# Hedgehog attention and a gated MLP on one core: projections on half rows of the array, and the tails' first layer with the tokens as weights

## The chip, the cores and the metric

The kernel runs on one NeuronCore of one Trainium2 chip. The metric is the device time of one execution in microseconds, the median of several. Three runs of the kernel before took 282.17, 283.19 and 283.45 us; the median is 283.19 us. The core has a tensor engine (PE, with its weight loads listed as PEld), VectorE (DVE), ScalarE (ACT), GpSimd (POOL) and SyncE (SP, which here only issues DMAs). A matmul takes its stationary operand from a weight load (`lhsT`), streams the moving operand (`rhs`) and writes into PSUM, of which this kernel uses eight buffers, one bank each.

## The reference, cut to what matters

There are 8 batches, 8 heads, 576 tokens, a head dimension of 64, 128 features, a model width of 512 and an inner width of 1024.

```python
def phi(x):
    proj = np.einsum('bhsd,df->bhsf', x, w_phi)
    proj = proj - np.max(np.abs(proj), axis=-1, keepdims=True)
    return np.concatenate([np.exp(proj), np.exp(-proj)], axis=-1)
q_p, k_p = phi(q), phi(k)
kv = np.einsum('bhsf,bhsd->bhfd', k_p, v);  z = np.sum(k_p, axis=2)
num = np.einsum('bhsf,bhfd->bhsd', q_p, kv)
den = np.einsum('bhsf,bhf->bhs', q_p, z)[..., None] + 1e-06
x = (num / den).transpose(0, 2, 1, 3).reshape(B, S, H * D)
h = np.maximum(x @ w_in, 0.0)
u, v = h[..., :d_ff // 2], h[..., d_ff // 2:]
v_n = (v - mean(v)) / np.sqrt(var(v) + 1e-06)
v_s = np.einsum('ts,bsd->btd', w_spatial, v_n) + b_spatial[None, :, None]
out = (u * v_s) @ w_out
```

## The kernel before, in words

**Units.** Of the 576 tokens of a batch, 512 are taken as four blocks of 128 (`NB`), and the last 64 are a tail. The attention works in 36 units: 32 of two heads of one batch (`pair`), and four tail units, which hold the tails of two batches side by side, 64 rows each (`TL = 64`), for all eight heads. In each unit there are eight groups of 128 rows by 64 dimensions: two heads by four blocks, or eight heads of the tails.

**One unit.** The keys and queries of a unit are brought into transposed form (`kT`, `qT`): four tiles of 128 x 128, in which rows 0 to 63 hold the dimensions of one group and rows 64 to 127 those of the next. For batches from 2 on a DMA transposes them (`cross`), before that PE does (`a_transpose`). `by_token` (L263) multiplies them with `wphi2`, a block diagonal matrix of 128 x 256: `w_phi` stands in rows 0 to 63 of the left half and in rows 64 to 127 of the right half, and the rest is zero. So one matmul over all 128 rows gives the projections of two groups, and two matmuls fill a PSUM bank. `a_keys` (L270) takes the largest absolute value of each projection on DVE (L278) and both exponentials on ACT (L281). `a_queries` (L283) takes the queries' maxima (L292) and splits each into two bf16 numbers in `mhl`. `a_scale` makes the values times the exponentials of the keys' maxima (`vs`, POOL). Later steps of the same unit turn the maxima (`a_max_t`, L327), project the queries again by feature with the maxima taken off (`a_qfeat`, L344 to L365), sum keys and values (`a_kv`, L378 to L383), divide (`a_num`, L398, with L388 and L389) and turn the result into `xT` (`a_x_t`).

**The MLP.** For each batch `b_v` makes the `v` half of the first layer by token (`v_mm`, L447, with its evacuation L449 and statistics L450 and L451), `b_root` and `b_ln` normalize it (L461, L467), `b_u` makes the `u` half by feature (L534, L536), `b_s` does the spatial product and the gate (L543, L544, L546) and `b_o` the output product (`o_mm`, L568, L571). The tails of a batch go through the same steps in functions of their own. `b_v_tail` (L488) computes all eight 128-wide slices of the first layer for the 64 tail tokens, with the weights stationary and the tokens moving: 32 matmuls of 64 columns (L497). It evacuates the `v` slices to `vTt` (L499) and the `u` slices to `uTt` (L500). `b_turn_tail` (L502) turns `vTt` back with four transposes (L507), copies the result out of PSUM on DVE (L511) and takes its statistics (L512, L513).

**Order.** The program is written out step by step. Step i emits the stages of several units after one another (`ORDER`, with lags: the keys and queries of unit i, the sums of unit i-2, the attention of unit i-3, and so on). Behind the stages for keys, queries, sums and next, `fill` takes MLP tasks from a queue: each task has a cost, and each of these stages gives a share of a credit that follows from the length of the queue. `b_tasks` (L625) lists a batch's tasks in order. `load` and its relatives are emitted at given steps on the queues of SP and POOL. A scheduler then lays the instructions out for each engine and assigns the eight PSUM banks. It may move an instruction a few places. Each engine works through its own list in order.

**Around the change.** In step i the keys' four projections come first, then their readers, then MLP tasks for a credit share of 0.375, then the queries' four projections with their readers, and then MLP tasks for a share of 0.25. In PE's list that is the burst of the keys, one or two MLP groups, the burst of the queries, and a further group.

Of the kernel before, what the change touches and what calls it, by code (L numbers as in the profile page):

```python
# [8 lines left out]
FP32 = mybir.dt.float32  # L9
BF16 = mybir.dt.bfloat16  # L10
AF = mybir.ActivationFunctionType
ALU = mybir.AluOpType
AX = mybir.AxisListType
# [3 lines left out]
def kernel(  # L17
# [15 lines left out]
    nc = tc.nc  # L33

    B, H, S, D = q.shape
    F = w_phi.shape[1]
# [3 lines left out]
    P = 128  # L40
    KC = DM // P
# [3 lines left out]
    TL = S - T0  # L45
# [4 lines left out]
    cpool = ctx.enter_context(tc.tile_pool(name="const", bufs=1))  # L50
# [4 lines left out]
    s2 = ctx.enter_context(tc.tile_pool(name="stage_b", bufs=2))  # L55

    psum = ctx.enter_context(tc.tile_pool(name="psum", bufs=8, space=bass.MemoryType.PSUM))
# [14 lines left out]
    gs = {}  # L72
# [47 lines left out]
        pin(nc.sync.dma_start_transpose)(out=u[x + "T"], in_=src.rearrange("p h x -> p (h x)"))  # L120


    wphi_f = s2.tile([P, F], FP32, tag="ob", name="wphi_f", bufs=6)
    for i in range(2):
        pin(nc.scalar.dma_start)(out=wphi_f[i * D:(i + 1) * D, :], in_=w_phi)
    alloc(0)
# [12 lines left out]
    bias = cpool.tile([P, NB], FP32)  # L139
# [4 lines left out]
    ident = cpool.tile([P, P], BF16)  # L144
# [115 lines left out]
            u[x + "T"] = a1.tile([P, 4, P], BF16, tag="kT", name="kT") if x == "k" else qts[u["i"] % len(qts)]  # L260
            copy(out=u[x + "T"], in_=pt)

    def by_token(xT, half):  # L263
        ps = psum.tile([P, 4, F], FP32, tag="bank", name="ps")
        for x in range(2):
            nc.tensor.matmul(out=ps[:, 2 * x:2 * x + 2, :], lhsT=xT[:, 2 * half + x, :], rhs=wphi2,  # L266
                             start=True, stop=True)
        return ps

    def a_keys(u):  # L270

        u["mk"] = small.tile([P, H], FP32, tag="mk", name="mk")
        u["kf"] = feat.tile([P, 2, H, F], BF16, tag="kf" if u["pair"] else "kf_t", name="kf",
                            bufs=4 if u["pair"] else 2)
        for half in range(2):
            pk = by_token(u["kT"], half)
            hs = slice(4 * half, 4 * half + 4)
            nc.vector.tensor_reduce(out=u["mk"][:, hs], in_=pk, axis=AX.X, op=ALU.max,  # L278
                                    apply_absolute_value=True)
            for s, sc in ((0, 1.0), (1, -1.0)):  # L280
                nc.scalar.activation(out=u["kf"][:, s, hs, :], in_=pk, func=AF.Exp, bias=0.0, scale=sc)  # L281

    def a_queries(u):  # L283

        m, early = mhl[u["i"] % NM], u["i"] < EARLY
        if not early:
            mq = small.tile([P, H], FP32, tag="mq", name="mq")
        for half in range(2):
            pq = by_token(u["qT"], half)
            if early and half == 0:  # L290
                mq = pq[:, 0, 0:H]
            nc.vector.tensor_reduce(out=mq[:, 4 * half:4 * half + 4], in_=pq, axis=AX.X, op=ALU.max,  # L292
                                    apply_absolute_value=True)
        eng = nc.vector if early else nc.gpsimd
        eng.tensor_copy(out=m[:, 0:H], in_=mq)
        eng.tensor_tensor(out=m[:, H:2 * H], in0=mq, in1=m[:, 0:H], op=ALU.subtract)

    def a_scale(u):
        em = small.tile([P, 2, H], FP32, tag="em" if u["pair"] else "em_t", name="em", bufs=3 if u["pair"] else 1)
# [144 lines left out]
    def v_mm(lhs, dst, r, stats, mv):  # L444
        pv = psum.tile([P, HALF], FP32, tag="bank", name="pv")
        for kc in range(KC):
            nc.tensor.matmul(out=pv[r], lhsT=lhs(kc), rhs=w_in_bf[:, kc, HALF:DFF],  # L447
                             start=(kc == 0), stop=(kc == KC - 1))
        nc.scalar.activation(out=dst[r], in_=pv[r], func=AF.Relu, bias=0.0, scale=1.0)  # L449
        nc.vector.bn_stats(out=stats[r], in_=dst[r])  # L450
        nc.vector.bn_aggr(out=mv[r], in_=stats[r])  # L451
# [35 lines left out]

    def b_v_tail(g, bls):  # L488
        d = gs[g]
        if bls[0] == 0:  # L490
            d["uTt"] = s2.tile([P, KC, P], BF16, tag="uTt", name="uTt", bufs=2)
        d["vTt"] = s2.tile([P, KC, TL], BF16, tag="vr", name="vTt", bufs=5)
        r = slice(bls[0] * TL, (bls[-1] + 1) * TL)
        pu = psum.tile([P, 2 * KC, TL], FP32, tag="bank", name="pu")
        for dc in range(2 * KC):
            for kc in range(KC):
                nc.tensor.matmul(out=pu[:, dc, :], lhsT=w_in_bf[:, kc, dc * P:(dc + 1) * P],  # L497
                                 rhs=d["xTt"][:, kc, r], start=(kc == 0), stop=(kc == KC - 1))
        nc.scalar.activation(out=d["vTt"], in_=pu[:, KC:2 * KC, :], func=AF.Relu, bias=0.0, scale=1.0)  # L499
        nc.scalar.activation(out=d["uTt"][:, :, r], in_=pu[:, 0:KC, :], func=AF.Relu, bias=0.0, scale=1.0)  # L500

    def b_turn_tail(g, bls):  # L502
        d = gs[g]
        r = slice(bls[0] * TL, (bls[-1] + 1) * TL)
        pt = psum.tile([P, KC, P], BF16, tag="bank", name="pt")
        for dc in range(KC):
            nc.tensor.transpose(out=pt[r, dc, :], in_=d["vTt"][:, dc, :], identity=ident)  # L507
        vr = s2.tile([P, HALF], BF16, tag="vr", name="vr", bufs=5)
        stats = small.tile([P, 6], FP32, tag="stats", name="stats")
        mv = small.tile([P, 1, 2], FP32, tag="mv_t", name="mv_t")  # L510
        nc.vector.tensor_copy(out=vr[r], in_=pt[r].rearrange("p n e -> p (n e)"))  # L511
        nc.vector.bn_stats(out=stats[r], in_=vr[r])  # L512
        nc.vector.bn_aggr(out=mv[r, 0, :], in_=stats[r])  # L513
        d["ln"] = vr, moments(mv, r, 1)

    def b_root_tail(g, bls):
# [11 lines left out]
    def b_u(b, dc):  # L528
        d = st[b]
        if dc == 0:  # L530
            d["uT"] = s2.tile([P, KC, T0], BF16, tag="uT", name="uT", bufs=1)
        pu = psum.tile([P, T0], FP32, tag="bank", name="pu")
        for kc in range(KC):
            nc.tensor.matmul(out=pu, lhsT=w_in_bf[:, kc, dc * P:(dc + 1) * P], rhs=d["xT"][:, kc, :],  # L534
                             start=(kc == 0), stop=(kc == KC - 1))
        nc.scalar.activation(out=d["uT"][:, dc, :], in_=pu, func=AF.Relu, bias=0.0, scale=1.0)  # L536

    def b_s(b, dc):
        d = st[b]
# [74 lines left out]
    MM = KC * T0 / 2400.0  # L614
# [10 lines left out]
    def b_tasks(b):  # L625

        g, bl = b // 2, b % 2
        outs = out_tasks(b - 1) if b else []
        vs = [(MM, lambda j=j: b_v(b, j)) for j in range(NB)]
        us = [(MM, lambda dc=dc: b_u(b, dc)) for dc in range(KC)]  # L630
        ss = [(MS, lambda dc=dc: b_s(b, dc)) for dc in range(KC)]
        ns = [(0.0, lambda j=j: b_ln(b, j)) for j in range(NB)]
        ts = outs[:1] + [(MM, lambda: b_v_tail(g, [bl]))] + vs[:2]
        ts += [(MM / 4, lambda: b_turn_tail(g, [bl]))] + outs[1:2] + vs[2:]
        ts += [(0.0, lambda: b_root_tail(g, [bl])), (0.0, lambda: b_ln_tail(g, [bl])), (0.0, lambda: b_root(b))]
        if b == 0:
            ts += [(0.3, lambda i=i: transpose_spatial(i)) for i in range(NB + 2)]
        for y in range(NB):
            ts += ns[y:y + 1] + outs[2 + y:3 + y] + us[y:y + 1]
        ts += ss  # L640
        ts.append((MS / 2, lambda: b_s_tail(g, [bl])))
        return ts + (out_tasks(b) if b == B - 1 else [])

# [26 lines left out]
    def step(i):  # L670

        if i == 0:
            a_transpose(units[0])
        left = [p - i + 1 for p in lists if p >= i]
        rate[0] = min(MOST, sum(cost for cost, _ in queue) / left[0]) if left else MOST
        for what, share in ORDER:
            for u in units[max(0, i - 5):i + 2]:
                if u["i"] + lag(u, what) != i or (what in ("sums", "attention", "out") and not u["pair"]):
                    continue
                last = u["pair"] and u["pj"] == NP - 1  # L680
                if what == "keys":
                    a_keys(u)
                    a_scale(u)
                elif what == "sums":
                    a_kv(u)
                elif what == "queries":
                    a_queries(u)
                elif what == "next":
                    a_transpose(u)
                elif what == "maxima":  # L690
                    a_max_t(u)
                elif what == "out":
                    a_x_t(u)
                    if last:
                        finish_batch(u, tail_x_t)
                        queue.extend(b_tasks(u["b"]))
                elif what == "features":
                    a_qfeat(u)
                elif what == "attention":
                    a_num(u)  # L700
                    if last:
                        finish_batch(u, tail_num)
            fill(share)
# [87 lines left out]
```

## Time and profile before

| | |
|---|---|
| median of three runs | 283.19 us |
| the profiled execution | 283.19 us, of which 281.4 us are the span from first to last instruction |
| busy share of the span | PE 92%, PEld 62%, DVE 86%, ACT 77%, POOL 65% |
| mean granted PE clock | 0.994 |
| 30 to 232 us | PE busy for 193.4 us, DVE 185.6, ACT 171.9, POOL 152.0 of 202 |
| 232 to 256 us | PE 24.0, DVE 16.2, ACT 12.3 of 24 |
| the projections L266 | 288 matmuls of 128 x 256, 272 ns each from start to end |
| the tails' first layer L497 | 256 matmuls of 128 x 64, 193 ns each from start to end |
| maxima L278, L292; exponentials L281 | 680 and 677 ns; 624 ns |

One execution was recorded. Each line of an instruction view has the start in us from the beginning of the span, the duration of the group in us, the engine, the line of the kernel, what is written and read, the shapes and the number of instructions; in brackets the engine's idle time before it and what ended it. A matmul line carries the part of the array that it uses as rows\*columns: 128\*128 is the whole array, 128\*64 half of its columns, 64\*128 half of its rows. Matmuls are pipelined, so one that takes 272 ns from start to end hands the array on long before: for throughput the distances from start to start count. The windows view gives, for a stretch, its length and then each engine's busy time, with the number of instructions in brackets, the granted PE clock, the DMA engines' share and GB/s. A line of the waits view has who waited for whom, then the sum in us, how many times, and the longest. The chain that ended last is the chain of work followed back from the last instruction, each step to what released it.

### The profile page before, as it was taken

To read this page: it belongs to the slowest core of one execution; us is meant where nothing else is said; L and a number is where in the kernel's file an instruction comes from. 1 tells how busy PE (TensorE), PEld (TensorE's weight loads), DVE (VectorE), ACT (ScalarE), POOL (GpSimd) and SP (SyncE) were. 2 spreads that over 40 slices of the span, in tenths; PEclk is the share of its full clock that TensorE was granted. 3 is DMA by queue.
4 is the path that set the end of the run, shared out by engine and by line. 5 is a ranking of instruction groups with operands and counts; after the bars stand their busy time and mean duration, and the time that the engine had idled before them with its cause. 6 is when DMAs were issued, how large, how long until landed. Compare 5 with 4: busy or idle time off the path is not lost.

```text
span 281.4 us, 8437 instructions
## 1 busy us (share of the span) xinstructions
PE 257.9 (92%) x3179; PEld 175.7 (62%) x3179; DVE 240.7 (86%) x623; ACT 217.0 (77%) x501; POOL 183.9 (65%) x312
## 2 busy tenths in 40 slices
PE   3769999999997999999997999999997999999993
PEld 2457877776764668666764667656864766555442
DVE  7978999989999899998889998997899797565752
ACT  6888998887896997888796979897896976723501
POOL 5897899899677954897677964897447740610200
PEclk9988999999999999999999999999999999999999
DMA  7989999999999996989789997989643300220115
GB/s 202 223 225 147 143 151 102 174 209 181 176 213 196 259 234 83 228 164 189 131 134 193 240 204 106 173 193 221 124 94 103 83 5 37 77 78 37 75 41 186
DMA packets 84985, 42.45 MB, mean 151 GB/s; under 512 B 51856, under 2 KB 80464, under 8 KB 84944
## 3 DMA queue, kind: packets, MB, share of 16 engines
q1 hardware_dynamic: 60240, 30.82, 50.4%
q0 software_dynamic: 24400, 10.89, 34.1%
q8 instruction: 25, 0.41, 0.6%
q10 hardware_dynamic: 304, 0.20, 0.2%
q14 instruction: 16, 0.13, 0.2%
HBM read 32.85 MB, written 9.44 MB: 150 GB/s over the span
## 4 chain that ended last, share of the span: by engine, by line
PE 58%; DVE 22%; ACT 8%; issue 4%; POOL 3%; DMA 2%; SPq 1%; ACTq 0%; POOLq 0%; DVEq 0%
PE ps L543 10%; PE pu L534 7%; PE po L568 7%; PE ps L266 6%; DVE mk L278 4%; DVE stats L450 4%; PE pv L378 4%; PE pv L447 4%; ACT kf L281 4%; PE pn L398 3%; PE ps L544 2%; PE pq L344 2%; PE pu L497 2%; DVE mq L292 2%; DVE x L389 2%
## 5 line engine op out<-in xcount | busy, mean ns | idle before, releaser
L306 POOL TENSOR_TENSOR vs<-v_f,em 128x512 bf16<-128x512 f32 x64 | 65.5, 1044 | 32.0 <-ACT em L301 31.8
L281 ACT ACTIVATE kf<-ps 128x512 bf16<-128x512 f32 x144 | 75.0, 624 | 11.2 <-DVE mk L278 10.8
L365 ACT ACTIVATE qf<-pq 128x512 bf16<-128x512 f32 x128 | 66.5, 618 | 9.6 <-PE pq L344 6.8
L278 DVE TENSOR_REDUCE mk<-ps 128x4 f32<-128x512 f32 x72 | 46.2, 680 | 1.2 <-PE ps L266 0.7
L292 DVE TENSOR_REDUCE mq<-ps 128x4 f32<-128x512 f32 x62 | 40.0, 677 | 0.8 <-PE ps L266 0.5
L543 PE MATMUL ps<-w_spT,vn 128*128 128x512 bf16 x128 | 33.3, 379 | 0.7 <-DVE vn L467 0.7
L568 PE MATMUL po<-w_out_bf,uT 128*128 128x512 bf16 x124 | 31.7, 379 | 2.0 <-ACT kf L281 1.2
L534 PE MATMUL pu<-xT,w_in_bf 128*128 128x512 bf16 x128 | 32.1, 379 | 0.0
L461 POOL TENSOR_TENSOR rs<-var,neghalf 64x1 f32<-64x1 f32 (+1 forms) x16 | 12.7, 795 | 29.3 <-DVE var L456 29.0
L447 PE MATMUL pv<-w_in_bf,xT 128*128 128x512 bf16 x128 | 31.5, 379 | 0.0
L450 DVE BATCH_NORM_STATS2 stats<-vr 128x6 f32<-128x512 bf16 x32 | 21.6, 682 | 7.8 <-ACT vr L449 7.7
L378 PE MATMUL pv<-vs,kf 128*128 128x66 bf16 x512 | 24.5, 193 | 3.8 <-ACT kf L281 3.1
L546 DVE TENSOR_TENSOR uT<-ps,uT 128x512 bf16<-128x512 f32 x32 | 21.5, 686 | 6.7 <-PE ps L544 5.4
L378 PEld LDWEIGHTS <-kf 128*128 128x128 bf16 x512 | 21.8, 97 | 7.0 <-issue 5.8
L536 ACT ACTIVATE uT<-pu 128x512 bf16<-128x512 f32 x32 | 19.5, 629 | 7.7 <-PE pu L534 5.1
L389 DVE TENSOR_TENSOR x<-pn,rc 128x256 bf16<-128x256 f32 x64 | 24.9, 418 | 0.4
L398 PEld LDWEIGHTS <-qf 128*128 128x128 bf16 x512 | 20.2, 97 | 6.1 <-ACT qf L365 0.4
L449 ACT ACTIVATE vr<-pv 128x512 bf16<-128x512 f32 x32 | 19.7, 624 | 5.4 <-PE pv L447 4.9
L380 PE MATMUL pv<-vst,kf 128*128 128x66 bf16 x128 | 21.2, 191 | 1.9 <-POOL vst L61 1.9
L398 PE MATMUL pn<-kv,qf 128*128 128x66 bf16 x512 | 21.8, 193 | 0.4 <-ACT qf L365 0.3
L467 POOL TENSOR_SCALAR vn<-vr,rs 128x512 bf16<-128x512 bf16 x28 | 21.3, 771 | 0.9
L571 ACT COPY ob<-po 128x512 f32<-128x512 f32 x17 | 10.2, 600 | 15.0 <-PE po L568 15.0
(137 smaller groups left out, 580.1 us busy)
## 6 DMA issues: line engine op xcount, KB each, us to landing
out_dram<-ob SPq DMA_DIRECT2D x31, 256.0 KB, 2.9
v_f<-in_v_dram SPq DMA_DIRECT2D x14, 512.0 KB, 6.1
k_bf<-in_k_dram POOLq DMA_DIRECT2D x14, 256.0 KB, 5.6
q_bf<-in_q_dram POOLq DMA_DIRECT2D x14, 256.0 KB, 5.4
qt<-qT_b SPq DMA_DIRECT2D x24, 64.0 KB, 4.3
out_dram<-ob SPq DMA_DIRECT2D x9, 128.0 KB, 2.8
v_tl<-in_v_dram SPq DMA_DIRECT2D x8, 128.0 KB, 6.3
v_f<-in_v_dram SPq DMA_DIRECT2D x1, 1024.0 KB, 8.8
```

The costliest lines, as they stand in the source:

```text
L278: nc.vector.tensor_reduce(out=u["mk"][:, hs], in_=pk, axis=AX.X, op=ALU.max, apply_absolute_value=True)
L281: nc.scalar.activation(out=u["kf"][:, s, hs, :], in_=pk, func=AF.Exp, bias=0.0, scale=sc)
L292: nc.vector.tensor_reduce(out=mq[:, 4 * half:4 * half + 4], in_=pq, axis=AX.X, op=ALU.max, apply_absolute_value=True)
L306: nc.gpsimd.tensor_tensor(out=vs[:, s, :, 0:D], in0=st[u["b"]]["v"][:, pj * H:(pj + 1) * H, :], in1=em[:, s, :].unsqueeze(2).to_broadcast( ...
L365: nc.scalar.activation(out=qf[:, s], in_=pq, func=AF.Exp, bias=0.0, scale=sc)
L378: nc.tensor.matmul(out=pv[:, hh, s, :], lhsT=u["kf"][:, s, 4 * hh + c, :], rhs=u["vs"][:, s, 4 * hh + c, :], start=(c == 0), stop=False)
L398: nc.tensor.matmul(out=pn[:, pos, :], lhsT=u["qf"][hh][:, s, pos, :], rhs=d["kv"][:, 2 * u["pj"] + hh, s, :], start=(s == 0), stop=(s == 1))
L447: nc.tensor.matmul(out=pv[r], lhsT=lhs(kc), rhs=w_in_bf[:, kc, HALF:DFF], start=(kc == 0), stop=(kc == KC - 1))
L450: nc.vector.bn_stats(out=stats[r], in_=dst[r])
L534: nc.tensor.matmul(out=pu, lhsT=w_in_bf[:, kc, dc * P:(dc + 1) * P], rhs=d["xT"][:, kc, :], start=(kc == 0), stop=(kc == KC - 1))
L543: nc.tensor.matmul(out=ps, lhsT=d["vn"][:, sp, cs], rhs=w_spT[:, sp, 0:T0], start=(sp == 0), stop=False)
L568: nc.tensor.matmul(out=po[r], lhsT=lhs(dc), rhs=w_out_bf[:, dc, :], start=(dc == 0), stop=(dc == KC - 1))
```

## The change

The projections of keys and queries of a unit are now issued in one burst ahead of all their readers (`a_project`). Each 128-row matmul of 256 columns becomes two matmuls of 64 rows and 128 columns: rows 0 to 63 with the left half of `wphi2`, rows 64 to 127 with the right half, in turn and into two PSUM banks, one for even and one for odd groups. The zero blocks are not multiplied any more. The readers work by bank and so by parity, with strided views. In a step the queries' readers stay where they were, behind the MLP tasks of the keys' share, while their projections stand before those tasks.

The tails' first layer is split into two parts. The `v` half takes the tokens as the stationary operand and goes through `v_mm` like the other blocks, into 64 rows of the bank, so that no turn is needed; `b_turn_tail` is gone. The `u` half becomes a task of its own (`b_u_tail`), ahead of the spatial products, and `uTt` has one buffer instead of two. In the list of tasks a cost of MM/4 is removed and one of MM/2 added. The float copy of `w_phi` gets its own place instead of a slot of the output buffers.

```diff
-    wphi_f = s2.tile([P, F], FP32, tag="ob", name="wphi_f", bufs=6)
+    wphi_f = cpool.tile([P, F], FP32)
...
-    def by_token(xT, half):
-        ps = psum.tile([P, 4, F], FP32, tag="bank", name="ps")
-        for x in range(2):
-            nc.tensor.matmul(out=ps[:, 2 * x:2 * x + 2, :], lhsT=xT[:, 2 * half + x, :], rhs=wphi2,
-                             start=True, stop=True)
+    def by_token(xT):
+        ps = [psum.tile([P, 4, F], FP32, tag="bank", name="ps") for _ in range(2)]
+        for j in range(4):
+            for y in range(2):
+                r = slice(y * D, (y + 1) * D)
+                nc.tensor.matmul(out=ps[y][:, j, :], lhsT=xT[r, j, :], rhs=wphi2[r, y * F:(y + 1) * F],
+                                 start=True, stop=True)
         return ps
+
+    def parity(t, y):
+        return t.rearrange("p (j two) -> p j two", two=2)[:, :, y]
+
+    def a_project(u):
+        u["pk"], u["pq"] = by_token(u["kT"]), by_token(u["qT"])
 
     def a_keys(u):
...
-        for half in range(2):
-            pk = by_token(u["kT"], half)
-            hs = slice(4 * half, 4 * half + 4)
-            nc.vector.tensor_reduce(out=u["mk"][:, hs], in_=pk, axis=AX.X, op=ALU.max,
+        for y, pk in enumerate(u["pk"]):
+            nc.vector.tensor_reduce(out=parity(u["mk"], y), in_=pk, axis=AX.X, op=ALU.max,
                                     apply_absolute_value=True)
             for s, sc in ((0, 1.0), (1, -1.0)):
-                nc.scalar.activation(out=u["kf"][:, s, hs, :], in_=pk, func=AF.Exp, bias=0.0, scale=sc)
+                nc.scalar.activation(out=u["kf"][:, s].rearrange("p (j two) f -> p j two f", two=2)[:, :, y, :],
+                                     in_=pk, func=AF.Exp, bias=0.0, scale=sc)
 
     def a_queries(u):
...
-        for half in range(2):
-            pq = by_token(u["qT"], half)
-            if early and half == 0:
-                mq = pq[:, 0, 0:H]
-            nc.vector.tensor_reduce(out=mq[:, 4 * half:4 * half + 4], in_=pq, axis=AX.X, op=ALU.max,
-                                    apply_absolute_value=True)
+        for y, pq in enumerate(u["pq"]):
+            nc.vector.tensor_reduce(out=mq[:, 4 * y:4 * y + 4], in_=pq, axis=AX.X, op=ALU.max, apply_absolute_value=True)
         eng = nc.vector if early else nc.gpsimd
-        eng.tensor_copy(out=m[:, 0:H], in_=mq)
-        eng.tensor_tensor(out=m[:, H:2 * H], in0=mq, in1=m[:, 0:H], op=ALU.subtract)
+        hi, lo = (m[:, e * H:(e + 1) * H].rearrange("p (j two) -> p two j", two=2) for e in range(2))
+        mq = mq.rearrange("p (two j) -> p two j", two=2)
+        eng.tensor_copy(out=hi, in_=mq)
+        eng.tensor_tensor(out=lo, in0=mq, in1=hi, op=ALU.subtract)
...
     def b_v_tail(g, bls):
         d = gs[g]
-        if bls[0] == 0:
-            d["uTt"] = s2.tile([P, KC, P], BF16, tag="uTt", name="uTt", bufs=2)
-        d["vTt"] = s2.tile([P, KC, TL], BF16, tag="vr", name="vTt", bufs=5)
         r = slice(bls[0] * TL, (bls[-1] + 1) * TL)
-        pu = psum.tile([P, 2 * KC, TL], FP32, tag="bank", name="pu")
-        for dc in range(2 * KC):
-            for kc in range(KC):
-                nc.tensor.matmul(out=pu[:, dc, :], lhsT=w_in_bf[:, kc, dc * P:(dc + 1) * P],
-                                 rhs=d["xTt"][:, kc, r], start=(kc == 0), stop=(kc == KC - 1))
-        nc.scalar.activation(out=d["vTt"], in_=pu[:, KC:2 * KC, :], func=AF.Relu, bias=0.0, scale=1.0)
-        nc.scalar.activation(out=d["uTt"][:, :, r], in_=pu[:, 0:KC, :], func=AF.Relu, bias=0.0, scale=1.0)
-
-    def b_turn_tail(g, bls):
...
-        for dc in range(KC):
-            nc.tensor.transpose(out=pt[r, dc, :], in_=d["vTt"][:, dc, :], identity=ident)
...
-        nc.vector.tensor_copy(out=vr[r], in_=pt[r].rearrange("p n e -> p (n e)"))
-        nc.vector.bn_stats(out=stats[r], in_=vr[r])
-        nc.vector.bn_aggr(out=mv[r, 0, :], in_=stats[r])
+        v_mm(lambda kc: d["xTt"][:, kc, r], vr, r, stats, mv[:, 0, :])
         d["ln"] = vr, moments(mv, r, 1)
...
+    def b_u_tail(g, bls):
+        d = gs[g]
+        if bls[0] == 0:
+            d["uTt"] = s2.tile([P, KC, P], BF16, tag="uTt", name="uTt", bufs=1)
+        r = slice(bls[0] * TL, (bls[-1] + 1) * TL)
+        pu = psum.tile([P, KC, P], FP32, tag="bank", name="pu")
+        for dc in range(KC):
+            for kc in range(KC):
+                nc.tensor.matmul(out=pu[:, dc, r], lhsT=w_in_bf[:, kc, dc * P:(dc + 1) * P],
+                                 rhs=d["xTt"][:, kc, r], start=(kc == 0), stop=(kc == KC - 1))
+        nc.scalar.activation(out=d["uTt"][:, :, r], in_=pu[:, :, r], func=AF.Relu, bias=0.0, scale=1.0)
...
-        ts = outs[:1] + [(MM, lambda: b_v_tail(g, [bl]))] + vs[:2]
-        ts += [(MM / 4, lambda: b_turn_tail(g, [bl]))] + outs[1:2] + vs[2:]
+        ts = outs[:1] + [(MM, lambda: b_v_tail(g, [bl]))] + vs[:2] + outs[1:2] + vs[2:]
...
-        ts += ss
+        ts += [(MM / 2, lambda: b_u_tail(g, [bl]))] + ss
...
                 if what == "keys":
+                    a_project(u)
                     a_keys(u)
                     a_scale(u)
```

More of the change, by code (lines that the diff above doesn't have):

```diff
@@ L274, in a_keys @@
                             bufs=4 if u["pair"] else 2)
-        for half in range(2):
-            pk = by_token(u["kT"], half)
-            hs = slice(4 * half, 4 * half + 4)
-            nc.vector.tensor_reduce(out=u["mk"][:, hs], in_=pk, axis=AX.X, op=ALU.max,
+        for y, pk in enumerate(u["pk"]):
+            nc.vector.tensor_reduce(out=parity(u["mk"], y), in_=pk, axis=AX.X, op=ALU.max,
                                     apply_absolute_value=True)
             for s, sc in ((0, 1.0), (1, -1.0)):
-                nc.scalar.activation(out=u["kf"][:, s, hs, :], in_=pk, func=AF.Exp, bias=0.0, scale=sc)
+                nc.scalar.activation(out=u["kf"][:, s].rearrange("p (j two) f -> p j two f", two=2)[:, :, y, :],
+                                     in_=pk, func=AF.Exp, bias=0.0, scale=sc)
     def a_queries(u):
         m, early = mhl[u["i"] % NM], u["i"] < EARLY
-        if not early:
+        if early:
+            mq = u["pq"][0][:, 0, 0:H]
+        else:
             mq = small.tile([P, H], FP32, tag="mq", name="mq")
-        for half in range(2):
-            pq = by_token(u["qT"], half)
-            if early and half == 0:
-                mq = pq[:, 0, 0:H]
-            nc.vector.tensor_reduce(out=mq[:, 4 * half:4 * half + 4], in_=pq, axis=AX.X, op=ALU.max,
-                                    apply_absolute_value=True)
+        for y, pq in enumerate(u["pq"]):
+            nc.vector.tensor_reduce(out=mq[:, 4 * y:4 * y + 4], in_=pq, axis=AX.X, op=ALU.max, apply_absolute_value=True)
         eng = nc.vector if early else nc.gpsimd
-        eng.tensor_copy(out=m[:, 0:H], in_=mq)
-        eng.tensor_tensor(out=m[:, H:2 * H], in0=mq, in1=m[:, 0:H], op=ALU.subtract)
+        hi, lo = (m[:, e * H:(e + 1) * H].rearrange("p (j two) -> p two j", two=2) for e in range(2))
+        mq = mq.rearrange("p (two j) -> p two j", two=2)
+        eng.tensor_copy(out=hi, in_=mq)
+        eng.tensor_tensor(out=lo, in0=mq, in1=hi, op=ALU.subtract)
     def a_scale(u):
@@ L489, in b_v_tail @@
         d = gs[g]
-        if bls[0] == 0:
-            d["uTt"] = s2.tile([P, KC, P], BF16, tag="uTt", name="uTt", bufs=2)
-        d["vTt"] = s2.tile([P, KC, TL], BF16, tag="vr", name="vTt", bufs=5)
         r = slice(bls[0] * TL, (bls[-1] + 1) * TL)
-        pu = psum.tile([P, 2 * KC, TL], FP32, tag="bank", name="pu")
-        for dc in range(2 * KC):
-            for kc in range(KC):
-                nc.tensor.matmul(out=pu[:, dc, :], lhsT=w_in_bf[:, kc, dc * P:(dc + 1) * P],
-                                 rhs=d["xTt"][:, kc, r], start=(kc == 0), stop=(kc == KC - 1))
-        nc.scalar.activation(out=d["vTt"], in_=pu[:, KC:2 * KC, :], func=AF.Relu, bias=0.0, scale=1.0)
-        nc.scalar.activation(out=d["uTt"][:, :, r], in_=pu[:, 0:KC, :], func=AF.Relu, bias=0.0, scale=1.0)
-    def b_turn_tail(g, bls):
-        d = gs[g]
-        r = slice(bls[0] * TL, (bls[-1] + 1) * TL)
-        pt = psum.tile([P, KC, P], BF16, tag="bank", name="pt")
-        for dc in range(KC):
-            nc.tensor.transpose(out=pt[r, dc, :], in_=d["vTt"][:, dc, :], identity=ident)
         vr = s2.tile([P, HALF], BF16, tag="vr", name="vr", bufs=5)
```

## The prediction

> **What bounds the kernel now.** I read the page first (shares of the engines and the chain that ended last), then the busy times of the stretch from 30 to 232 us, in which the attention units run, then what TensorE (PE) waits for, then the instructions in order of time around one unit, around a change of the array's mode, and at the end.
>
> ```profile
> PE 257.9 (92%) x3179; PEld 175.7 (62%) x3179; DVE 240.7 (86%) x623; ACT 217.0 (77%) x501; POOL 183.9 (65%) x312
> ...
> PE 58%; DVE 22%; ACT 8%; issue 4%; POOL 3%; DMA 2%; SPq 1%; ACTq 0%; POOLq 0%; DVEq 0%
> PE ps L543 10%; PE pu L534 7%; PE po L568 7%; PE ps L266 6%; DVE mk L278 4%; DVE stats L450 4%; PE pv L378 4%; PE pv L447 4%; ACT kf L281 4%; PE pn L398 3%; PE ps L544 2%; PE pq L344 2%; PE pu L497 2%; DVE mq L292 2%; DVE x L389 2%
> ```
>
> PE carries 58% of the chain, VectorE (DVE) 22%. The projections (L266) hold 6% of the span on the chain, 16.9 us, and the tails' first layer (L497) 2%, 5.6 us. From 30 to 232 us:
>
> ```profile
> 30.00:232.00 202.00, 193.41 (x2521) 135.07 (x2519) 185.58 (x474) 171.91 (x408) 152.01 (x260) 1.00 0.99 164
> ```
>
> PE is idle for 8.6 of 202 us, DVE for 16.4, ScalarE (ACT) for 30. PE binds, but DVE stands right behind it. What PE waits for, in the waits view:
>
> ```profile
> PE pv L378 <- ACT kf L281: 3.1, 2, 1.6
> ...
> PE po L568 <- ACT kf L281: 1.2, 1, 1.2
> PE po L568 <- DVE x L389: 0.9, 2, 0.6
> ...
> PE ps L266 <- DVE x L389: 0.6, 2, 0.5
> PE ps L266 <- DVE ob L571: 0.6, 1, 0.6
> ```
>
> None of these readers makes an operand of the matmul that waits: kf feeds L378 only two units later. They are the last readers of a PSUM bank that PE wants again. So 6.4 us of PE's waiting is for one of the eight banks.
>
> **Projections, per unit (36 of them).** PE in order of time, one unit:
>
> ```profile
> 174.70 1.02 PE L447 MATMUL pv<-w_in_bf,xT 128*128 128x512 bf16 x4
> 175.66 0.41 PE L507 MATMUL pt<-ident,vTt 128*64 128x128 bf16 x4
> 176.00 1.04 PE L568 MATMUL po<-w_out_bf,uT 128*128 128x512 bf16 x4
> ...
> 177.38 0.60 PE L266 MATMUL ps<-wphi,kT_b 128*128 128x256 bf16 x4
> 177.81 1.89 PE L447 MATMUL pv<-w_in_bf,xT 128*128 128x512 bf16 x8
> 179.54 0.60 PE L266 MATMUL ps<-wphi,qT_b 128*128 128x256 bf16 x4
> ```
>
> Start to start counts, since the ends overlap. The keys' four matmuls take 177.81-177.38 = 0.43, the queries' the same: 0.87 us a unit, 31.3 us in all. A full-array 128x512 matmul takes 1.73/8 = 0.216. Leaving the 128*128 mode costs time: four such matmuls should hand over after 0.86, at 175.56, and L507 starts at 175.66, 0.10 later. Coming back costs as much: four transposes of 128 columns at 0.056 are 0.22, and the next starts after 0.34, 0.11 later.
>
> After the change a unit has 16 matmuls of 64 rows and 128 columns, two at a time if both halves of the array run together. No row shows two row halves together; the nearest shows two column halves:
>
> ```profile
> 56.89 0.41 PE L236 MATMUL pt<-ident,wsp 128*64 128x128 bf16 x8
> 57.23 0.22 PE L236 MATMUL pt<-ident,wspt 64*64 64x64 bf16 x2
> ```
>
> Eight transposes hand over after 0.34, exactly as L507's four, which lie in one column half: pairs cost what singles cost. Bounds for the burst: paired 0.10+8x0.056+0.11 = 0.66, unpaired 0.10+16x0.056+0.11 = 1.11. I take the paired end: its row differs only in which side of the array is halved. Gain 0.21 a unit, 7.6 us of PE; at the other end +0.24, 8.6 us lost.
>
> The Trainium skill speaks against the full gain here: "TensorE: Matmul & The Clock Gate", Part 3, gives 3.07x for four row tiles, not 4x, and "TensorEngine Tiling (Array Packing)", Restrictions and Gotchas, warns that row tiling raises PSUM pressure. At the same efficiency two tiles would give 1.54x, the burst 0.79 and the gain 0.08 a unit, 2.9 us instead of 7.6, as an estimate. L236 shows no such loss for column halves; no row shows row halves.
>
> The readers keep their sizes: maxima 0.68, exponentials 0.62. The exponentials now write four blocks of 128 with gaps; ACT's copy of wphi into every other block of wm (L61, 128x512) takes 615 ns, so I charge nothing. The first keys' bank is complete after the seventh matmul instead of the second, about 0.1 later; DVE waited for L266 only 1.2 us in all, nothing charged.
>
> **Tails' first layer, eight half groups.** Out: 32 matmuls of 64 columns (L497, 0.93 in the chain of waits) and four transposes with both switches (0.44): 1.37. In: four 128x512 matmuls onto 64 output rows, 0.86 plus both switches 0.21, and 16 of 64 columns, 0.47: 1.54. PE +0.17 each, +1.4 us. DVE loses the copy L511, 8 x 0.42 = 3.4 us. ACT writes 64x512 (0.62 by L449) instead of 128x256 (0.41 by L499): +0.2 each, with 30 us of idle ACT to hide it; if that cover went it would cost 1.7. Queued behind that instruction are the next evacuations, for whose banks PE waits.
>
> **Small edits, charged nothing.** wphi_f leaves the output buffers for a place of its own; the first output group is at 75 us, long after. uTt has one buffer; its last reader, the tail's output product, stands two groups ahead of the new writer. No DMA is added or moved, and the order of SP, POOL and ACT is otherwise the old one.
>
> **The queries' burst ahead of the MLP groups.** Two more banks are wanted 1.73 us sooner (179.54 against 177.81) and held until DVE has reduced the keys. Cost per unit: below, -0.1 if DVE finds its operands ready (it waited 0.5 us for the queries' maxima from 30 to 232 us); above, +1.73 if no other bank is free. I take it into the discount below.
>
> **The end.** The last batch waits for its normalized rows:
>
> ```profile
> 263.92 2.75 PE L534 MATMUL pu<-xT,w_in_bf 128*128 128x512 bf16 x12
> ...
> 266.82 0.71 PE L543 MATMUL ps<-w_spT,vn 128*128 128x512 bf16 x2 [0.16 <-DVE vn L467]
> ...
> 267.61 0.73 DVE L467 TENSOR_SCALAR vn<-vr,rs 128x512 bf16<-128x512 bf16 x2
> 268.07 0.71 PE L543 MATMUL ps<-w_spT,vn 128*128 128x512 bf16 x2 [0.53 <-DVE vn L467]
> ```
>
> L534 should hand over at 263.92+12x0.216 = 266.51; L543 starts 0.31 late, and its third matmul 0.82 late (268.07 against 267.25): 1.13 us. DVE gets there 0.43 sooner without L511, and its first statistics come sooner too. PE has the tail's 0.47 to do in that gap and 0.30 less to do before it (1.07 against 1.37). Net -1.13+0.47-0.30 = -1.0 us.
>
> **Sum.** Of the projections' 31.3 us, 16.9 lie on the chain, 54%: 7.6 x 0.54 = -4.1. Of L497's 7.4, 5.6: 1.4 x 0.76 = +1.1. Of the statistics' DVE row (L450, 21.6 busy, 4% or 11.0 on the chain) half: the copy beside them gives -1.7. Together -4.7 in the middle. What is late next there is DVE, 92% busy, and the banks; PE has 8.6 us of slack, DVE 16.4, so I keep half, -2.4. With the end's -1.0: -3.4. The profiled execution took 283.19 around a span of 281.4, and 283.19 is also the median of the three runs: 283.2-3.4 = **279.8**.
>
> **Rivals.**
> - **PE keeps everything.** -7.6+1.4 on PE, and the end's wait 1.13 filled: -7.3, **275.9**. For it: PE's idle time is only 4% of the middle stretch. Against: DVE's 8% is not much more.
> - **The bank wait takes the place of the gain (slower).** Place: the burst, and the MLP group right behind it, which often gets the bank of the maxima's transpose (L327) just ahead of the burst. The named bank waits are 0.5 to 1.6 us long. One of 1.0 us in every sixth unit is +6.0: 283.2-3.4+6.0 = **285.8**. It decides from 3.4/36 = 0.09 us a unit. For it: 6.4 us of bank waits already. Against: most units show none.
> - **The halves do not pair (the change does not do what it says).** 8.6 x 0.54 = +4.6, tails and copy -0.6 halved to -0.3, the end -1.0: +3.3, **286.5**. Against: L236.
> - **DVE takes over at once.** The middle gives nothing, the end -1.0: **282.2**, no change.
>
> **Chances.** About 0.5% is what a measurement of this kernel can tell from no change: 281.8 to 284.6. Forecast 0.48 (own range 278.0 to 281.9; 0.45 faster, 0.03 same); PE keeps everything 0.14 (faster); bank wait 0.20 (0.17 slower, 0.03 same); no pairing 0.08 (slower); DVE 0.10 (same). Faster 0.59, same 0.16, slower 0.25. The range reaches from the full gain, 275.9, to just past the halves that do not pair, 287.0; beyond it are some bank waits over 1 us in every fifth unit.
>
> **What would show it.** The 16 matmuls of a unit start to start in 0.66 (right) or 1.11 (no pairing); DVE's share from 30 us on above 92% (right); idle PE before the burst or before the group behind it, released by evacuations (bank rival); no L511 and no wait of L543 at the end (right). I am wrong if the burst is short and the time is not: then the banks or DVE took the gain back.

## The result, and the profile after

The changed kernel takes 279.06 us (median of 278.16, 278.93, 279.20 and 279.21) against 283.09 beside it: ratio 0.9856, 95% interval 0.9824 to 0.9888. The forecast was 279.8. The profiled execution took 279.21 us around a span of 277.4. All ratios below are to the kernel before on the same chip; 0.0035 is 1 us.

The shares and the chain of the kernel after, from its page:

```profile
PE 255.0 (92%) x3339; PEld 164.6 (59%) x3339; DVE 236.3 (85%) x615; ACT 218.8 (79%) x501; POOL 183.7 (66%) x312
...
PE 46%; DVE 21%; ACT 10%; POOL 9%; DMA 8%; issue 4%; SPq 2%; POOLq 0%; DVEq 0%; ACTq 0%
PE ps L543 9%; PE po L568 7%; PE pu L522 6%; ACT kf L287 5%; PE pv L454 5%; DVE mk L284 5%; POOL vs L313 4%; PE pv L385 3%; DVE stats L457 3%; DMA qT_b<-q_bf 2%; PE ps L544 2%; DVE mq L298 2%; PE ps L268 2%; PE pn L405 2%; DMA v_tl<-in_v_dram 2%
```

The projections (now L268) went from 6% of the chain to 2%, yet no single item took their place: the 12% that PE lost on the chain are spread over DMA, POOL and ACT. The stretch from 30 to 232 us in the windows view of the kernel after:

```profile
30.00:232.00 202.00, 192.71 (x2701) 125.98 (x2699) 184.09 (x474) 175.77 (x412) 151.86 (x260) 1.00 1.12 165
```

PE 192.7, DVE 184.1: hardly moved. Busy shares do not show where the gain came from. One unit with a disturbed burst, and then one with an undisturbed one, on PE in the order of time:

```profile
174.92 0.40 PE L268 MATMUL ps<-wphi,kT_b 64*128 64x128 bf16 x8
175.15 0.39 PE L268 MATMUL ps<-wphi,qT_b 64*128 64x128 bf16 x8
176.19 1.89 PE L454 MATMUL pv<-w_in_bf,xT 128*128 128x512 bf16 x8 [0.65 <-DVE ob L571]
...
188.79 0.22 PE L334 MATMUL pt<-ident,mhl 128*128 128x128 bf16 x1
188.94 0.40 PE L268 MATMUL ps<-wphi,kT_b 64*128 64x128 bf16 x8
189.17 0.39 PE L268 MATMUL ps<-wphi,qT_b 64*128 64x128 bf16 x8
189.49 0.64 PE L534 MATMUL pu<-xTt,w_in_bf 128*128 128x64 bf16 x16
```

Undisturbed, the burst takes 189.49-188.94 = 0.55, and 0.10 to enter the mode (188.94-188.79 less 0.056): 0.65, forecast 0.66. In the trace two halves start 3 to 4 ns apart and the next pair 56 ns later, so they pair completely. In the first unit the MLP group behind the burst waits for a bank that an output copy on DVE still reads. The end:

```profile
260.74 2.75 PE L522 MATMUL pu<-xT,w_in_bf 128*128 128x512 bf16 x12
...
262.20 1.06 DVE L474 TENSOR_SCALAR vn<-vr,rs 128x512 bf16<-128x512 bf16 x3 [1.40 <-POOL rs L469]
...
263.33 0.63 PE L534 MATMUL pu<-xTt,w_in_bf 128*128 128x64 bf16 x16
...
263.80 1.03 PE L543 MATMUL ps<-w_spT,vn 128*128 128x512 bf16 x4
```

L543 no longer waits for vn; the tail's L534 fills the gap. From the last unit's first maximum to the end of the span it is 54.1 us instead of 55.2: -1.1.

### The profile page after: what moved, and what is told of

It reads as the page before. It is cut to its first block, busy times and chain, and to the rows that moved or that the text cites. A ratio compares the mean times of both kernels' runs of the same rounds, so it can differ in the third digit from the quotient of the medians.

```text
span 277.4 us, 8772 instructions
## 1 busy us (share of the span) xinstructions
PE 255.0 (92%) x3339; PEld 164.6 (59%) x3339; DVE 236.3 (85%) x615; ACT 218.8 (79%) x501; POOL 183.7 (66%) x312
## 4 chain that ended last, share of the span: by engine, by line
PE 46%; DVE 21%; ACT 10%; POOL 9%; DMA 8%; issue 4%; SPq 2%; POOLq 0%; DVEq 0%; ACTq 0%
PE ps L543 9%; PE po L568 7%; PE pu L522 6%; ACT kf L287 5%; PE pv L454 5%; DVE mk L284 5%; POOL vs L313 4%; PE pv L385 3%; DVE stats L457 3%; DMA qT_b<-q_bf 2%; PE ps L544 2%; DVE mq L298 2%; PE ps L268 2%; PE pn L405 2%; DMA v_tl<-in_v_dram 2%
## 5 line engine op out<-in xcount | busy, mean ns | idle before, releaser
L543 PE MATMUL ps<-w_spT,vn 128*128 128x512 bf16 x128 | 32.9, 380 | 0.0
L457 DVE BATCH_NORM_STATS2 stats<-vr 128x6 f32<-128x512 bf16 (+1 forms) x40 | 26.6, 683 | 7.0 <-ACT vr L456 6.4
L456 ACT ACTIVATE vr<-pv 128x512 bf16<-128x512 f32 (+1 forms) x40 | 23.6, 613 | 7.2 <-PE pv L454 6.9
```

Source lines behind the costliest of these rows:

```text
L543: nc.tensor.matmul(out=ps, lhsT=d["vn"][:, sp, cs], rhs=w_spT[:, sp, 0:T0], start=(sp == 0), stop=False)
```

## The experiments

The total was right, but that says nothing about its terms. Theory at the start: PE's saving and DVE's saving each count for about half, as forecast. Rivals: the projections or the tails alone give it all; and, formed when the two parts had been run alone: DVE sets the pace (D), the planner's new costs give a better order (P), the loads set the pace (L).

A ledger is used throughout. From the first maximum of the tenth unit to that of the last, PE's time is matmuls, mode changes and waits. A wait is what lies between two starts beyond what the first matmul takes alone and 0.095 us for a mode change, if it is over 0.02 us; it is worked out from the starts in the trace. "At the bursts" are those ahead of a projection and of the matmul right behind it. In f1, f2 and f3 some PE records are missing, so only the bursts are listed. The ledger is that of one execution each: those of e4 and e5 took 1.0 and 1.1 us less than their medians, that of f2 0.6 more.

| kernel | ratio, 95% | stretch us | waits at the bursts (times) | waits elsewhere |
|---|---|---|---|---|
| before | 1 | 176.5 | 3.7 (11) | 7.2 |
| e1 projections alone | 0.9956 (0.9932 to 0.9981) | 175.6 | 7.1 (20) | 7.9 |
| e2 tails alone | 0.9861 (0.9837 to 0.9885) | 173.8 | 1.7 (5) | 4.9 |
| e4 one burst, whole rows | 0.9903 (0.9881 to 0.9926) | 175.2 | 2.8 (12) | 4.9 |
| e5 half rows, two bursts | 0.9913 (0.9887 to 0.9939) | 174.8 | 0.6 (4) | 7.0 |
| after | 0.9856 (0.9824 to 0.9888) | 174.5 | 5.0 (14) | 7.1 |
| f1 after, more DVE | 0.9935 (0.9910 to 0.9960) | 176.2 | 7.1 (21) | |
| f2 before, turn on ACT | 0.9945 (0.9918 to 0.9972) | 176.2 | 1.5 (6) | |
| f3 before, other cost | 1.0021 (0.9998 to 1.0044) | 177.0 | 4.0 (12) | |
| f5 after, fewer DVE copies | 0.9801 (0.9774 to 0.9827) | 173.4 | 4.1 (13) | 7.0 |

**The two parts alone.** e1 is the kernel before with the change's `by_token`, `a_project` and readers; e2 is the kernel before with the change's tail functions and its list of tasks. In both `wphi_f` stays where it was.

> The kernel before with the projections of the change alone (half rows, one burst ahead of all readers); the tails stay as before. My theory: PE's 7.6 us are saved, but only the second half of the run and the end are paced by PE; 280.6 us. Rival A (the tails' part brings most of the gain): 282.0 or more. Rival B (the bursts' bank waits eat the gain): 282.5 or more, with idle PE just behind the bursts. If everything came from the projections: 279.1.

> The kernel before with the tails' part of the change alone; projections as before. My theory: 1.0 us at the end by the lost wait for the normalized rows, and 0.4 by the eight copies that DVE no longer makes; 281.7 us. Rival A (the tails bring most): 280.0 or less. Rival C (the tails' extra 0.17 us of PE each cost as much as they give): 283.0.

e1 281.12 us, e2 278.74, before 282.48. The tails alone give 3.9 us (3.3 to 4.6), as much as the whole change; the projections give 1.2 alone (0.5 to 1.9), and 0.1 on top of the tails (within 1.1 either way). e2 is what rival A expected; e1 lies between the theory and A. The waits views of PE from 44 to 228 us, first before, then e1, then e2:

```profile
PE pv L378 <- ACT kf L281: 3.1, 2, 1.6
PE po L568 <- ACT kf L281: 1.2, 1, 1.2
PE po L568 <- DVE x L389: 0.9, 2, 0.6
PE ps L266 <- DVE x L389: 0.6, 2, 0.5
PE ps L266 <- DVE ob L571: 0.6, 1, 0.6
```

```profile
PE pv L385 <- ACT kf L287: 3.4, 5, 1.4
PE ps L268 <- DVE x L396: 2.1, 4, 0.8
PE po L575 <- ACT kf L287: 1.1, 1, 1.1
PE po L575 <- DVE x L396: 0.6, 1, 0.6
PE ps L268 <- DVE ob L578: 0.6, 1, 0.6
```

```profile
PE pv L378 <- ACT kf L281: 1.1, 1, 1.1
PE po L561 <- ACT kf L281: 0.8, 1, 0.8
PE pv L447 <- ACT kf L281: 0.6, 1, 0.6
PE ps L266 <- ACT qf L365: 0.5, 1, 0.5
```

In e1 the projections wait 2.1 us for DVE's normalization (x) to give a bank back, 0.6 before; in e2 PE waits for DVE in none of these lines. By the ledger: e1 saves 26 units x 0.21 = 5.5 us of PE and pays 3.4 more in waits at the bursts and 0.7 elsewhere; the stretch is 0.9 shorter. After against e2: 5.5 saved, 3.3 + 2.2 back in waits; the stretch is no shorter (+0.7).

**The projections' two sides.** e4 is the kernel after with whole-row matmuls in its one burst; e5 puts the queries' half-row burst back behind the MLP groups.

```diff
 e5: def a_project(u):
-        u["pk"], u["pq"] = by_token(u["kT"]), by_token(u["qT"])
+        u["pk"] = by_token(u["kT"])
 e5: def a_queries(u):
+        u["pq"] = by_token(u["qT"])
```

> The kernel after with whole rows again (four matmuls of 256 columns each for keys and queries, no change of mode), but in one burst ahead of all readers; tails as after. It differs from the tails alone only in the place of the queries' projections. My theory: the place costs or gives little, within 0.7 us of the tails alone, 281.0 to 282.4. Rival B (banks): at least 1.5 us slower than the tails alone, 283.2 or more. If the earlier queries help DVE: 280.5 or less.

> The kernel after, but with the queries' projections back at their old place behind the MLP tasks: half rows in pairs, two bursts a unit, so two more changes of mode (0.2 us) per unit, 7.2 us of PE. My theory: about half of that is paid, 279.1 + 3.0 = 282.1. Rival B (banks): the changes of mode are paid back by the banks, 279.5 or less.

Both 280.0 us. The expectation for e4 counted with 281.7 us for the tails alone, so its distance from e2 decides, not its time. e4 against e2 is the new order, and the new place of `wphi_f`, which was not run alone: +1.2 us (0.3 to 2.1), between the theory's 0.7 and rival B's 1.5, with 1.1 us more waits at the bursts. After against e4 is the half rows alone: -1.3 us (0.2 to 2.4). e5 is 1.6 us above after (0.5 to 2.8), where 3.0 were expected: it loses nearly all waits at the bursts (0.6 us) but pays for four mode changes a unit instead of two. One of its bursts:

```profile
127.94 0.22 PE L335 MATMUL pt<-ident,mhl 128*128 128x128 bf16 x1
128.09 0.40 PE L268 MATMUL ps<-wphi,kT_b 64*128 64x128 bf16 x8
128.42 0.64 PE L535 MATMUL pu<-xTt,w_in_bf 128*128 128x64 bf16 x16
```

0.33 from start to next and 0.10 to enter, twice, are 0.86, what whole rows cost. That explains why the half rows gain nothing in e5, but not why e5 is 1.5 us slower than e2, whose MLP groups fall around the bursts in the same places; PE's waits elsewhere are 7.0 us against 4.9, and the reason stays open. So the pairing needs the one burst, and the one burst needs two more banks at once and the queries' operands earlier. Both show in the waits view of the kernel after, from 44 to 228 us:

```profile
PE pv L385 <- ACT kf L287: 1.5, 2, 1.2
PE ps L268 <- DMA qT_b<-q_bf: 0.7, 1, 0.7
...
PE po L568 <- DVE mT L340: 0.7, 2, 0.4
PE pv L454 <- DVE ob L571: 0.7, 1, 0.7
...
PE ps L268 <- DVE qt L261: 0.5, 2, 0.3
```

qT_b and qt are the queries themselves, not banks: the DMA and the copy that bring them now end later than PE wants them, 1.2 us in all.

**Order of the halves.** e3 is the kernel after with four matmuls of one half issued ahead of four of the other (`for y` outside `for j`).

> The kernel after with the eight matmuls of one row half first and then the eight of the other, four and four per tensor, so that neighbours sit in the same half and cannot run together. My theory (the pairs are the gain): a burst takes 1.0 to 1.1 us instead of 0.64 from start to start, 16 us of PE more, about half of it paid: 285 to 288 us. If the pairs run together anyway at the seam, or if the burst's length is not what counts: 280 or less.

278.63 us, ratio 0.9876 (0.9838 to 0.9915): no difference from after. The run does not show what unpaired halves would cost, because the array overlapped the halves anyway. One unit of e3:

```profile
189.75 0.41 PE L268 MATMUL ps<-wphi,kT_b 64*128 64x128 bf16 x8
189.98 0.40 PE L268 MATMUL ps<-wphi,qT_b 64*128 64x128 bf16 x8
190.32 0.64 PE L534 MATMUL pu<-xTt,w_in_bf 128*128 128x64 bf16 x16
```

0.57 us from start to next, 0.02 more than with the halves in turn. The two of a pair now start 13 to 19 ns apart instead of 3 to 4, so the order did change, and the premise that these neighbours cannot run together was wrong: the second half does not wait for the four that stand ahead of it.

**Loads (L).** e6 is before, e7 after, and both leave loads out.

> The kernel before, but from batch 2 on the keys, queries and values of batch b-2 are used again, so that 36 of 48 of these loads and their issues on POOL and SP are left out (its output is that of other inputs). My theory: in the first half of the run the loads and POOL set the pace beside PE; 278 to 281 us. Rival D (DVE is next to PE): the loads do not matter, 282.5 or more.

> The kernel after with the same loads left out as in the run before it, whose time it is to be set against. My theory: with the loads gone the saved PE time shows in the first half too, and the distance to the kernel before without these loads grows from 4.0 to 5.5 us or more. Rival D (DVE takes the rest): the distance stays at 4.0 or less. Rival B (banks): as D, and idle PE behind the bursts stays.

e6 284.03 us, 1.0074 (1.0045 to 1.0104); e7 279.29, 0.9869 (0.9827 to 0.9912). Neither is faster than the kernel that it was made from. From the tenth unit on, e6's units start within 0.2 us of those of before. The distance between e6 and e7, for which the second expectation was put, is 4.7 us by the medians and 5.8 by the ratios, but it grew because e6 became slower, not because e7 became faster. So L falls as far as loads from memory go; the DMAs that transpose keys and queries stayed in. Why e6 is 2 us slower is open.

**DVE or the planner (D, P).** f1 adds a DVE operation to each tail half group of the kernel after; f2 moves the turn's copy of the kernel before from DVE to ACT; f3 changes only the turn's cost in `b_tasks`.

```diff
 f1, behind v_mm in b_v_tail:
+        nc.vector.tensor_scalar(out=idle[r], in0=vr[r], scalar1=neghalf[r, 0:1], scalar2=neghalf[r, 1:2], ...)
 f2, in b_turn_tail:
-        nc.vector.tensor_copy(out=vr[r], in_=pt[r].rearrange("p n e -> p (n e)"))
+        nc.scalar.copy(out=vr[r], in_=pt[r].rearrange("p n e -> p (n e)"))
 f3, in b_tasks:
-        ts += [(MM / 4, lambda: b_turn_tail(g, [bl]))] + ...
+        ts += [(MM / 2, lambda: b_turn_tail(g, [bl]))] + ...
```

> The changed kernel, and in each of the eight tail half groups VectorE does one more operation of 64x512 (into a spare buffer that nobody reads), about 0.4 us, as long as the copy that the change took away; no work is left out. If VectorE sets the pace of the middle, so that the copies that went counted nearly in full: 281 to 282 us, 2 to 3 us more than the changed kernel's 279.1. If the gain came from the order in which the planner now gives out the MLP's groups, or from the turn as such (its banks, its waits, its changes of the array's mode): 279.1 to 279.8.

> The kernel before, with the evacuation of the tails' turned rows on ScalarE instead of VectorE (3.4 us of VectorE in all). If VectorE's copies are what the change gained by: 280 to 280.7 us. If the planner's order or the turn itself is: 282.4 to 283.2, as before. ScalarE's own queue speaks for a little loss in either case.

> The kernel before, with the planner's cost of the tails' turn MM/2 instead of MM/4: the sum of costs per batch is then the one of the changed kernel, and the MLP's groups fall into the units as there; no instruction is added or left out. If the new order of the groups is what the tails' part gained by: 279.5 to 281 us. If VectorE's copy or the turn itself is: 282.4 to 283.2, as before.

f1 280.59 us, f2 280.97, f3 283.41, before 282.89. f3 gains nothing, so the higher sum of costs is not it. But it does not give the order of the changed kernel: by the traces the MLP groups fall around the bursts as in e2 in only 8 of 26 units, fewer than in before itself (12), since the new task also stands elsewhere in the list. So P is excluded as to the costs, not as to the order.

In f2 the groups fall as in before in all 26 units, and in f1 as in after: these two change no order. f2 gains 1.6 us (0.8 to 2.3) from 3.4 us of DVE, though ACT has 8 x 0.58 = 4.6 more to do, and the waits at the bursts fall from 3.7 to 1.5. If anything this is too little. The granted clock (third number from the end) halved for 3.5 us in its profiled execution, inside the stretch:

```profile
213.50:217.00 3.50, 3.28 (x26) 1.85 (x26) 1.97 (x6) 2.13 (x7) 3.50 (x5) 0.51 0.27 91
```

At its 29th unit, earlier than this, f2 is 2.4 us ahead of the kernel before (after: 2.7); at the last unit only 1.1. Four of its twelve executions had a mean granted clock of 0.986 and took 281.6 to 282.9 us; the other eight, at 0.991 and more, have a mean of 280.6, which is 2.2 us below the 282.7 of before at such clocks.

f1 loses 2.2 us against after (1.1 to 3.4), and the waits at the bursts rise from 5.0 to 7.1. Its dose was larger than meant, as its group shows (count, then busy us and mean ns):

```profile
L503 DVE TENSOR_SCALAR vr<-vr,neghalf 64x512 bf16<-64x512 bf16 x8 | 5.8, 720 | 0.0
```

Five of the eight take 0.39 to 0.41, three 0.92, 1.08 and 1.77. So DVE time counts for some 2.2/5.8 = 0.38 where it is added (f1; 0.2 to 0.6 by the interval) and 1.6/3.4 = 0.46 where ACT takes it over (f2; 0.2 to 0.7).

**A dose for PE.** f4 is the kernel after with every burst's matmuls issued twice.

```diff
-        for j in range(4):
+        for j in [*range(4), *range(4)]:
```

> The changed kernel, with the sixteen half-row matmuls of every burst issued twice (the second time over the first, same values): TensorE works 0.45 us more in each of 36 units, 16 us in all, and the readers of the projections get them 0.45 us later. If TensorE sets the pace, so that the projections' saving was only given back elsewhere: +8 us or more (287 and up). If the projections' time is converted as in the run with the projections' part alone (about a sixth): at most +3, 280 to 282.

288.72 us, 1.0227 (1.0199 to 1.0255): 10.5 us above after for 16 us of PE, as the first expectation had it. It was not paid evenly. Start of the first maximum of a unit, against the same unit of before, from the three traces:

| unit | 10th | 21st | 29th | last |
|---|---|---|---|---|
| before, us | 49.7 | 123.1 | 179.7 | 226.2 |
| after | -0.8 | -0.6 | -2.7 | -2.8 |
| f4 | -1.1 | +0.4 | +2.7 | +5.8 |

By the 21st unit f4 has issued 9 us more on PE and is 1 us behind after; from there to the last, 15 units x 0.45 = 6.8 us cost 7.6. So PE time that is added is paid in full in the second part of the stretch, and there is slack for it in the first. What sets the pace in the first, the runs do not say; loads do not (e6, e7). PE time that is saved is not paid back in full in the second part either: from the 21st unit to the last e1 saves 15 x 0.21 = 3.2 us of PE and gains 0.8. So PE does not set the pace there alone. f4 also hands the projections to their readers 0.45 us later, which it does not separate from PE's time.

**A version that follows from D.** f5 is the kernel after with 13 instead of 18 of the output copies on DVE.

```diff
-        turn[0] ^= 1
-        (nc.vector.tensor_copy if turn[0] else nc.scalar.copy)(out=ob[r], in_=po[r])
+        turn[0] += 1
+        on_dve = turn[0] % 3 == 0 if turn[0] <= 27 else turn[0] % 2
+        (nc.vector.tensor_copy if on_dve else nc.scalar.copy)(out=ob[r], in_=po[r])
```

> The changed kernel, with every third instead of every second of the first 27 output evacuations on VectorE (9 instead of 14) and the others on ScalarE, which is 79% busy: about 3 us less on VectorE, as much more on ScalarE. If VectorE still sets the pace at the rate of the run with the added VectorE operation (about two thirds): 277 us, 2 less than the changed kernel. If TensorE has become the bound in its place, so that work taken from either engine alone buys little while work added to either costs most of its time: 278.5 to 279.5. If ScalarE is as near its bound: 280 or more.

277.18 us against 282.94, 0.9801 (0.9774 to 0.9827): the fastest of all, 1.6 us below after (0.4 to 2.7) for 5 x 0.68 = 3.4 us of DVE, again 0.46, as the first expectation had it. The MLP groups fall as in after. Between the two profiled executions 1.1 us lie in the stretch, and as much again ahead of the tenth unit, where no output copy has run yet. From 30 to 232 us in f5:

```profile
30.00:232.00 202.00, 193.22 (x2713) 126.29 (x2711) 181.57 (x472) 177.97 (x417) 152.92 (x262) 1.00 1.04 165
```

DVE is down to 181.6 while ACT, at 178.0 of 202, still takes the copies without loss.

## Why the prediction was right, and where it was not

The sum was right by luck: two errors cancelled. Its own sign of being wrong, "the burst is short and the time is not", is what the projections show on top of the tails; the tails' gain hid it.

- **The burst: right.** 0.65 us measured, 0.66 forecast; the halves pair. The Trainium skill's "TensorE: Matmul & The Clock Gate", Part 3, gives 3.07x for four row tiles; two row tiles here lose nothing, so the 0.79 us estimated by it was too long. The warning in its "TensorEngine Tiling (Array Packing)", Restrictions and Gotchas, that row tiling raises PSUM pressure, holds here for the one burst only: the waits at the bursts are 5.0 us against 2.8 with whole rows (after, e4), but in two bursts 0.6 against 1.7 (e5, e2).
- **The projections' term: too large.** "7.6 x 0.54 = -4.1", halved to about -2, was -1.2 alone and -0.1 on top of the tails. The step that failed stands under the queries' burst: two more banks, put at -0.1 to +1.73 a unit and taken "into the discount". The new order costs 1.2 us (e4 against e2, the place of `wphi_f` included), and by the ledger the 5.5 us that after saves against e2 come back as 3.3 us of waits at the bursts and 2.2 elsewhere.
- **The share on the chain was the wrong factor.** 54% says how much of L266 lay on one chain. It does not say what shortening it is worth where the next matmul waits for a bank. f4 shows the other face: more PE costs two thirds of its length.
- **The tails: too small.** -0.6, halved, plus -1.0 at the end made -1.3; e2 gives -3.9. The added PE time, "+1.1", is not seen: PE's waits in the stretch fall by 4.3 us (10.9 to 6.6). Of the copy's "-1.7" the forecast kept half; f2 shows 1.6 (2.2 at the higher clock), so by that run nothing of it should have been taken off. Some 1.3 us remain (3.9 less 1.6 by the copy, less 1.0 at the end, of which f2 may hold a part), or 0.7 with the 2.2. The sum of the planner's costs is excluded; whether the new order of the MLP groups, the turn's bank, its waits or its mode changes made the rest was not tried alone.
- **The end: right.** -1.0 forecast, -1.1 in the profile of after.
- **"DVE's share from 30 us on above 92%": wrong.** It is 184.09/202 = 91%. DVE did not become fuller; by the waits at the bursts in f1 and f2 it mattered as the engine that gives banks back late.
- **The bank rival: right in kind, not in size.** Waits at the bursts rose, by 3.4 us with the projections alone and 3.3 on top of the tails (26 units), not by 6. They took the projections' gain and no more, and of the waits of after 1.2 us are for the queries themselves, which this rival did not name.

## What to carry to other kernels

Where PE waits for PSUM banks, a microsecond saved on PE is worth what the next bank allows, and one saved on the engine that empties the banks can be worth more than its share of the chain says; here 0.4 to 0.5 of DVE's time (the intervals reach from 0.1 to 0.8) against 0.0 to 0.2 of what the projections saved on PE. Run the parts of a change alone even when the sum is right: the smaller-looking part, alone, gave as much as the whole. When a run is to test an order, compare the order in its trace: f3 had another one than was meant. Moving evacuations from the fuller to the emptier engine (f5) is the cheap test, and here the better kernel.

## What the runs showed of the hardware

- Two row halves of the array overlap in both orders that were run: 0.55 us with the halves in turn, where the two of a pair start 3 to 4 ns apart, and 0.57 with four of one ahead of four of the other, 13 to 19 ns apart.
- A change of the array's mode costs 0.09 to 0.10 us on entering and again on leaving; with four a unit instead of two the half rows take 0.86 us, as long as whole rows (e5).
- A DVE operation from SBUF to SBUF in bf16 lengthened beside GpSimd: f1's added operation took 0.41 us or less in five places, and 1.77 us where it began under two GpSimd multiplications; it ended 0.15 to 0.16 us after the second. Those of 0.92 and 1.08 us also end some 0.15 us after a GpSimd multiplication. That the two contend is read from these three places and was not tried by itself. First DVE, then GpSimd:

```profile
173.37 1.77 DVE L503 TENSOR_SCALAR vr<-vr,neghalf 64x512 bf16<-64x512 bf16 x1
```

```profile
172.94 2.05 POOL L61 TENSOR_TENSOR vst<-v_tl,em 64x512 bf16<-64x512 f32 x2
```
